# Three sines for four, a filter evacuated in 384 and 256 columns, an early table load, and a new time estimate and order for accumulating transfers in a gated long-convolution and token-mixer kernel

## The chip, the cores and the metric

The kernel runs on one core of one Trainium2 chip. The metric is the device time of one execution in microseconds (us). Before the change it took 180.29 us (median of 3 runs, 179.93 to 180.88). A profiled execution has a span some 2 us shorter than its time (177.7 and 179.50 us in the one profiled here). Each run also lists the mean clock granted to TensorE, as a share of full speed. Unless said, all runs told here are of the undisturbed (fast) state.

## The reference, cut to what matters

```python
x = A_q                                            # [1, 2048, 640], bf16
g = sigmoid((x * gate_w).sum(-1, keepdims=True))
# a: long convolution
kv = shift(k, shift_k) * v                         # 4-tap causal filter, then a product
y  = irfft(rfft(pad(kv)) * rfft(pad(ssm_k)))       # length 4096 per channel, first 2048 kept
a  = x * (y + kv * ssm_D)
# b: token mixer
b  = w2.T @ gelu(w1.T @ layernorm(x) + b1) + b2    # 2048 -> 1536 -> 2048 over the sequence
out = g * a + (1 - g) * b
```

## The kernel before

The Fourier transforms are matmuls against a basis of sines that the kernel computes itself (`FTB`), in four phases p, followed by additions on VectorE that combine the phases ("mixing"). A spectrum lies in four slots of 2560 columns of a tile `C[i]` or `SS`. The filter's spectrum (`W` evacuations) is made in two halves, then those of the two halves of kv. Products and cross sums of the spectra follow, then an inverse mixing and 64 + 64 inverse matmuls. TensorE fills all gaps with the mixer's two large matmuls: 384 of the first (`X,ring`), 384 of the second (`GT,W`).

All instructions are put down as operations in a list, with estimated durations. At build time a list scheduler simulates the engines, lets each take the ready operation of the lowest priority number, and so fixes the order in each engine's stream. On the chip each engine works through its stream in order, and stands at the first instruction whose operand isn't there. The scheduler's estimate for a transfer (those issued by GpSimd (POOL) accumulate: they add one tile to another while moving it):

```python
if e in ("SP", "QA") or op.lat < 0:                 # a transfer
    issue = 1.2 if e == "POOL" else 0.1
    s = max(t + issue, dma_free)
    dma_free = s + op.dur                           # one shared channel for all transfers
    op.end = dma_free + 2.0 + (6.0 if e == "POOL" else 0.0)   # accumulating ones land 6 us later
    free[e] = t + issue
```

The start of the kernel: four sines, five transposes of filter half one with spins (matmuls on a zero tile) ahead of them, and filter matmuls evacuated in 640 columns (2 x 320):

```python
for p in PORD:                                       # 0, 2, 1, 3
    t_ = tt("DVE", pv, V(tb, ...), V(jrow, 512 * p, ...), ALU.add)
    pprev = ts("DVE", pa, pa, 4095, None, ALU.bitwise_and, mode=4)
    sins[p] = act(FTB[:, p, ...], pa, ACT.Sin, bias=cst[:, 0:1], scale=..., name="sin")
...
def k_turn(hk):       # VectorE permutes a loaded block of k, a transfer then transposes it
    SC.add("DVE", 0.75, ... e.tensor_copy(ov, iv) ..., prio=0, name="kperm")
    dma(KT[hk // 2][...], o, 128 * 5120, rate=200.0, transpose=True, chain=True)
...
# the end: cross sums of the second half (A1), then the product of the first (A0)
acc_dma(A1[1], V1[1])                                # 2 accumulating transfers each
acc_dma(A1[0], V1[0])
chained(product, A0[1], A0[1], V0[1], H(V0[1], 0))   # ends with one more
lastacc = SC.ops[-1]
```

## Time and profile before

| | before |
|---|---|
| time, median of 3 (us) | 180.29 |
| span profiled (us), clock | 177.7, 1.000 |
| TensorE busy (us, share) | 172.6, 97% |
| VectorE busy | 169.7, 96% |
| ScalarE busy | 117.0, 66% |
| second mixer matmul starts (us) | 105.27 |
| VectorE's last mixing ends | 166.59 |

"Busy" is an engine's time in instructions. In the timelines below a row is: start, length, engine, line of the source, operation, output<-input with shapes, number of like instructions joined, and in brackets the idle time ahead of it and what ended it. In the lists of waits a row ends with the total, the number and the longest wait in us.

### The profile page before, as it was taken

Reading aid. Unit: us, or ns where it says so; the run is one execution under the profiler, and the core shown is the slowest. Engines: PE = TensorE matmul, PEld = TensorE weight load, DVE = VectorE, ACT = ScalarE, POOL = GpSimd, SP = SyncE. Lnnn points to the kernel's source line nnn. Section 1 sums busy time; section 2 is a strip of 40 time slices with the busy share of each in tenths; the row PEclk is TensorE's granted clock in tenths of the full one; section 3 lists DMA queues with packets and bytes.
Section 4 is the critical chain, followed back from the end, with each engine's and each line's share of the span. In section 5 each row is a group of like instructions: output and inputs, shape, how many; then the busy total and the mean of one; then the engine's idle time right before and its main releaser. Section 6 shows DMA issues by size and latency. Waiting matters only on the chain.

```text
span 177.7 us, 3342 instructions
## 1 busy us (share of the span) xinstructions
PE 172.6 (97%) x1380; PEld 129.4 (73%) x1381; DVE 169.7 (96%) x203; ACT 117.0 (66%) x176; POOL 43.6 (25%) x52
## 2 busy tenths in 40 slices
PE   7999999799999999999999999999999999999993
PEld 2666787487788776777777778888888887777772
DVE  7899789989999999999999999999999999999974
ACT  4999997998999999529999911231321323754760
POOL 8089803300000065000241101204343000252000
PEclk9999999999999999999999999999999999999999
DMA  4999999999999999999999998898999999499363
GB/s 136 394 411 374 391 312 156 248 414 374 191 240 315 109 216 226 231 228 278 230 227 271 205 248 299 144 225 230 188 193 217 207 218 408 167 197 212 93 241 131
DMA packets 38542, 43.51 MB, mean 245 GB/s; under 512 B 15867, under 2 KB 31360, under 8 KB 38528
## 3 DMA queue, kind: packets, MB, share of 16 engines
q1 hardware_dynamic: 33296, 32.16, 61.2%
q0 software_dynamic: 5200, 11.14, 36.5%
q8 instruction: 11, 0.18, 0.5%
q14 instruction: 3, 0.02, 0.0%
q10 hardware_dynamic: 32, 0.01, 0.0%
HBM read 25.87 MB, written 2.62 MB: 160 GB/s over the span
## 4 chain that ended last, share of the span: by engine, by line
PE 88%; DMA 5%; ACT 3%; SPq 2%; issue 0%; DVE 0%
PE pp L298 88%; DMA rows<-in_B_b_dram 5%; SPq L272 2%; ACT C L676 1%; ACT L676 1%; ACT GT L676 0%; DVE O L688 0%
## 5 line engine op out<-in xcount | busy, mean ns | idle before, releaser
L298 PE MATMUL pp<-X,ring 128*128 128x320 bf16 x384 | 55.3, 299 | 0.0
L632 DVE TENSOR_TENSOR C<-C 128x2560 bf16<-128x2560 bf16 (+2 forms) x37 | 54.5, 1523 | 0.8 <-ACT C L676 0.6
L298 PE MATMUL pp<-GT,W 128*128 128x320 bf16 x384 | 52.6, 299 | 0.0
L298 PEld LDWEIGHTS pp<-GT,W 128*128 128x128 bf16 x384 | 43.5, 113 | 8.7
L298 PEld LDWEIGHTS pp<-X,ring 128*128 128x128 bf16 x384 | 37.3, 98 | 14.3
L676 ACT ACTIVATE C<-pp 128x640 bf16<-128x640 f32 x64 | 40.7, 731 | 2.8 <-PE pp L298 2.7
L676 ACT ACTIVATE O<-pp,c,omg 128x640 bf16<-128x640 f32 x15 | 13.3, 885 | 34.7 <-PE pp L298 34.7
L267 POOL DMA_DIRECT2D C<-C x8 | 11.0, 1616 | 43.9 <-DVE C L632 43.9
L298 PE MATMUL pp<-wT,FTB 128*128 128x320 bf16 x112 | 17.1, 299 | 0.7 <-ACT GT L676 0.5
L676 ACT ACTIVATE cgb<-pp,gg 128x640 bf16<-128x640 f32 x16 | 12.7, 795 | 5.6 <-PE pp L298 5.2
L676 ACT ACTIVATE GT<-pp,cc 128x640 bf16<-128x640 f32 x12 | 9.6, 803 | 9.3 <-PE pp L298 9.2
L298 PEld LDWEIGHTS pp<-wT,FTB 128*128 128x128 bf16 x112 | 10.5, 98 | 5.6 <-ACT GT L676 0.8
L632 DVE TENSOR_TENSOR tm<-C,C 128x2560 bf16<-128x2560 bf16 (+1 forms) x7 | 14.3, 2059 | 0.0
L954 DVE BATCH_NORM_STATS2 stats<-X 128x6 f32<-128x320 bf16 x32 | 13.6, 464 | 0.5 <-DMA X<-in_A_q_dram 0.5
L298 PE MATMUL pp<-C,FTB 128*128 128x320 bf16 x96 | 13.4, 299 | 0.0
L267 POOL DMA_DIRECT2D C<-q_hi x6 | 5.9, 977 | 27.6 <-DVE C L632 12.9
L298 PEld LDWEIGHTS pp<-C,FTB 128*128 128x128 bf16 x96 | 9.4, 98 | 3.6
L676 ACT ACTIVATE gq<-gq 128x640 bf16<-128x640 bf16 x16 | 11.8, 745 | 0.2 <-DVE gq L632 0.2
L632 DVE TENSOR_TENSOR SS<-C 128x2560 bf16<-128x2560 bf16 x8 | 11.7, 1488 | 0.1
L632 DVE TENSOR_TENSOR C<-tm 128x2560 bf16<-128x2560 bf16 (+1 forms) x9 | 10.7, 1194 | 0.1
L676 ACT ACTIVATE ksh<-pp 128x1024 bf16<-128x1024 f32 (+1 forms) x12 | 9.9, 903 | 0.2 <-PE pp L298 0.2
L267 POOL DMA_DIRECT2D O<-q_hi x4 | 4.8, 1200 | 21.3 <-DVE q_hi L632 21.3
(77 smaller groups left out, 197.0 us busy)
## 6 DMA issues: line engine op xcount, KB each, us to landing
ring<-in_B_w_dram SPq DMA_DIRECT2D x12, 512.0 KB, 12.2
W<-in_B_w_dram SPq DMA_DIRECT2D x12, 512.0 KB, 5.5
C<-C POOLq DMA_DIRECT2D x8, 640.0 KB, 11.5
X<-in_A_q_dram SPq DMA_DIRECT2D x4, 640.0 KB, 8.4
kn<-in_A_k_dram SPq DMA_DIRECT2D x4, 640.0 KB, 9.4
out_dram<-O SPq DMA_DIRECT2D x7, 320.0 KB, 3.4
C<-SS POOLq DMA_DIRECT2D x3, 640.0 KB, 11.9
ssm<-in_A_ssm_k_dram SPq DMA_DIRECT2D x3, 512.0 KB, 6.8
```

What stands on the lines that cost most here:

```text
L267: ins = engobj.dma_start(out_ap, in_ap, accum_op=ALU.add, max_dma_last_dim=2560)
L272: ins = engobj.dma_start(out_ap, in_ap)
L298: ins = self.nc.tensor.matmul(ps_ap, lhsT=lhsT, rhs=rhs, start=start, stop=stop, skip_group_check=True)
L632: o_ = SC.add(eng, d, lambda s: T.op(eng, lambda e: e.tensor_tensor(o, a, b, op), rd, [o]), rd, [o], prio=prio, name="tt")
L676: return T.op("ACT", lambda e: e.activation(o, src, func, **kw), rr + [src], ww)
L954: ops.append(SC.add("DVE", 0.38, (lambda o, i: lambda s: T.op("DVE", lambda e: e.bn_stats(o, i), [i], [o]))(o, i), [i], [o]))
```

## The change

Its intent: shorten the start, which ScalarE bounds (one sine less, the basis of phases 0 and 2 from one sine by copies and negations; fewer evacuations), take the gelu table's load out of a queue where TensorE waits for it, place the first two turns of k where their loads have landed, and order the accumulating transfers of the end so that the first cross sum needed isn't queued behind others. Cut to its core:

```diff
-                    s = max(t + issue, dma_free)
-                    dma_free = s + op.dur
-                    op.end = dma_free + 2.0 + (6.0 if e == "POOL" else 0.0)
+                    if e == "POOL":
+                        acc_free = max(t + issue + 0.6, acc_free) + 2.2 * op.dur
+                        op.end = acc_free
+                    else:
+                        s = max(t + issue, dma_free)
+                        dma_free = s + op.dur
+                        op.end = dma_free + 2.0
...
-        SPIN = (7, 3, 3, 2, 2)
+        SPIN = (7, 2, 1, 1, 1)
...
-            sins[p] = act(FTB[:, p, ...], pa, ACT.Sin, ...)            # x4
+            sins[(0, 1, 3)[n_]] = act(so, si, ACT.Sin, ...)            # x3
+        sins[2] = sins[0]
+        for o_, i_, sg in (...):                                       # 4 scalings by -1 or 1
+            h_ = ts("DVE", V(FTB, o_[0], ...), V(FTB, i_[0], ...), sg, None, ALU.mult, mode=4)
...
+            if ci == 1:          # one evacuation of 4 x 256 columns per phase
+                ... wT[:, kt, p, 384:640] ...
-                items.append((chk(c), ..., srcW(0)(kt, p, ci), ...))   # 320 columns
+                items.append((..., wT[:, kt, p, 0:384], ...))          # 384 columns
...
+                g_ = act(gws[:, :], cst[:, 1:2], ACT.Gelu_apprx_tanh, name="tab", prio=SC.ops[-1].idx)
+                g_.after.add(SC.ops[-2])
...
+                        if t in (13, 15):
+                            kpos.append(b1)
                     k_turn(hk)
+                    SC.ops[-2].after.add(kpos[hk])
...
+        n_acc = len(SC.ops)
         acc_dma(A1[1], V1[1])
         acc_dma(A1[0], V1[0])
         chained(product, A0[1], A0[1], V0[1], H(V0[1], 0))
         lastacc = SC.ops[-1]
+        for o_ in SC.ops[n_acc:]:
+            if o_.eng == "POOL" and o_ is not lastacc:
+                o_.after.add(lastacc)
```

Below, "the new model" is the first hunk and "the reorder" the last; the rest are "the early parts".

More of the change, by code (lines that the diff above doesn't have):

```diff
@@ L405, in run @@
         dma_free = 0.3
+        acc_free = 0.0
         avail = {}
@@ L809, in _build @@
         iota(acol[:, :], [[0, 1]], 0, 8)
-        jr = lambda p, kt: iota(jrow[:, 2 * p + kt, :], [[-512 * (4 * kt + p), 2], [4 * (4 * kt + p), 128]], 4096 + 4 * kt + p, 0)
-        for p in PORD:
-            for kt in range(2):
-                jr(p, kt).dur = 0.34
-            if p == PORD[0]:
-                iota(dif[:, :], [[1, 128]], 0, -1)
+        for k_, j in enumerate((0, 4, 2, 6)):
+            iota(jrow[:, k_, 0:128], [[4 * j, 128]], 4096 + j, 0).dur = 0.23
+        iota(dif[:, :], [[1, 128]], 0, -1)
+        for k_, j in enumerate((1, 5, 3, 7)):
+            iota(jrow[:, 4 + k_, :], [[-512 * j, 2], [4 * j, 128]], 4096 + j, 0).dur = 0.34
         iota(dif2[:, :], [[1, 32]], 128, -1)
@@ L823, in _build @@
         sins = {}
-        for p in PORD:
-            pv = V(pint, 1024 * p, [[512, 2], [256, 2], [1, 256]])
-            t_ = tt("DVE", pv, V(tb, 0, [[0, 2], [256, 2], [1, 256]]), V(jrow, 512 * p, [[256, 2], [0, 2], [1, 256]]), ALU.add)
-            if p != 0:
+        pprev = None
+        for n_ in range(3):
+            pa = V(pint, 1024 * n_, [[1, 1024]])
+            if n_ == 0:
+                t_ = tt("DVE", V(pint, 0, [[256, 4], [128, 2], [1, 128]]), V(tb, 0, [[0, 4], [256, 2], [1, 128]]), V(jrow, 0, [[256, 4], [0, 2], [1, 128]]), ALU.add)
+            else:
+                t_ = tt("DVE", V(pint, 1024 * n_, [[512, 2], [256, 2], [1, 256]]), V(tb, 0, [[0, 2], [256, 2], [1, 256]]), V(jrow, 1024 + 512 * (n_ - 1), [[256, 2], [0, 2], [1, 256]]), ALU.add)
                 t_.after.add(pprev)
-            pa = pint[:, p, :, :, :].rearrange("q a b c -> q (a b c)")
             pprev = ts("DVE", pa, pa, 4095, None, ALU.bitwise_and, mode=4)
-            if p == 0:
+            if n_ == 0:
                 ts("DVE", ident[:, :], dif[:, :], 0.0, None, ALU.is_equal)
-            sins[p] = act(FTB[:, p, :, :, :, :].rearrange("q a b c d -> q (a b c d)"), pa, ACT.Sin, bias=cst[:, 0:1],
-                scale=-(2.0 * math.pi / 4096.0) * (1.0 - 1e-6), name="sin")
+            so = V(FTB, 0, [[2048, 2], [256, 4], [1, 128]]) if n_ == 0 else V(FTB, 1024 * (1, 3)[n_ - 1], [[1, 1024]])
+            si = V(pint, 0, [[512, 2], [128, 4], [1, 128]]) if n_ == 0 else pa
+            sins[(0, 1, 3)[n_]] = act(so, si, ACT.Sin, bias=cst[:, 0:1], scale=-(2.0 * math.pi / 4096.0) * (1.0 - 1e-6), name="sin")
+        sins[2] = sins[0]
+        half_rows = []
+        for o_, i_, sg in (((640, 256), (512, 256), -1.0), ((128, 256), (0, 256), 1.0), ((2432, 256), (2048, 768), -1.0), ((2176, 768), (2304, 256), 1.0)):
+            h_ = ts("DVE", V(FTB, o_[0], [[o_[1], 2], [1, 128]]), V(FTB, i_[0], [[i_[1], 2], [1, 128]]), sg, None, ALU.mult, mode=4)
+            h_.after.add(pprev)
+            half_rows.append(h_)
         SC.add("DVE", 0.6, lambda s: T.op("DVE", lambda e: e.tensor_copy(ro, ri), [ri], [ro]), [ri], [ro], prio=0, name="taps")
@@ L872, in transp @@
             m_ = mms(vt, (spin(SPIN[db]) if h == 0 else []) + items, name="wtr")
-            m_.dur = (0.65 + 0.31 * SPIN[db] if h == 0 else 0.55)
+            m_.dur = (1.9 if db == 0 else 0.65 + 0.31 * SPIN[db]) if h == 0 else 0.55
             o_ = act(V(wT, 2 * h * SL + 128 * db, [[SL, 2], [D, 4], [1, 128]]), (lambda s: s[:, :].rearrange("q (a b c) -> q a b c", a=2, b=4)), ACT.Copy, vt=vt, name="wT")
             if h == 0:
-                o_.after.add(sins[0 if db == 0 else 2])
+                o_.after.add(sins[1 if db < 3 else 3])
+                if db == 2:
+                    sins[3].after.add(o_)
         def fwd_c(p, ci, dst, scale):
+            if ci == 1:
+                vt = _VT("cv")
+                items = []
+                for k2 in range(2):
+                    for c in range(2):
+                        for kt in range(2):
+                            items.append(((lambda s, j=2 * c + k2: s[:, 256 * j:256 * j + 256]), FTB[:, p, kt, c, k2, :], wT[:, kt, p, 384:640], kt == 0, kt == 1))
+                m_ = mms(vt, items, name="W")
+                m_.dur = 0.88
+                act(V(dst, p * SL + 384, [[D, 4], [1, 256]]), lambda s: s[:, :].rearrange("p (a f) -> p a f", a=4), ACT.Copy, vt=vt, name="We", scale=scale)
+                return
             for k2 in range(2):
@@ L883, in fwd_c @@
                     for c in range(2):
-                        items.append((chk(c), FTB[:, p, kt, c, k2, :], srcW(0)(kt, p, ci), kt == 0, kt == 1))
+                        items.append(((lambda s, c=c: s[:, 512 * c:512 * c + 384]), FTB[:, p, kt, c, k2, :], wT[:, kt, p, 0:384], kt == 0, kt == 1))
                 m_ = mms(vt, (spin(WSPIN) if (p, ci, k2) == (PORD[0], 0, 0) else []) + items, name="W")
-                m_.dur = 0.54
-                act(V(dst, p * SL + k2 * D + 320 * ci, [[2 * D, 2], [1, 320]]), two, ACT.Copy, vt=vt, name="We", scale=scale)
+                m_.dur = 0.66
+                act(V(dst, p * SL + k2 * D, [[2 * D, 2], [1, 384]]), lambda s: s[:, :].rearrange("p (c f) -> p c f", c=2)[:, :, 0:384], ACT.Copy, vt=vt, name="We", scale=scale)
         def fwd(src, h, p, dst, slot, scale, name, neg=lambda c, k2: False):
@@ L956, in ln_tile @@
                 ops[0].after.add(pprev)
+                ops[0].after.update(half_rows)
             o, i = mv[:, t, :], stats[:, t, :]
@@ L979, in _build @@
         KFP = (0, 5, 10, 15)
-        WSPIN = 3
+        WSPIN = 1
         srcW = lambda h: (lambda kt, p, ci: wT[:, 2 * h + kt, p, 320 * ci:320 * ci + 320])
@@ L986, in _build @@
                 consts()
+            else:
+                g_ = act(gws[:, :], cst[:, 1:2], ACT.Gelu_apprx_tanh, name="tab", prio=SC.ops[-1].idx)
+                g_.dur = 1.5
+                g_.after.add(SC.ops[-2])
             if h in (1,):
@@ L1008, in _build @@
                 pag = []
+                kpos = []
                 def flush():
```

## The prediction

> **What bounds the kernel now.** I read the page first. On the page of the kernel before, the shares of each engine and the chain that ended last say this (busy microseconds, share, instructions; then the chain's shares by engine):
>
> ```profile
> PE 172.6 (97%) x1380; PEld 129.4 (73%) x1381; DVE 169.7 (96%) x203; ACT 117.0 (66%) x176; POOL 43.6 (25%) x52
> ...
> PE 88%; DMA 5%; ACT 3%; SPq 2%; issue 0%; DVE 0%
> ```
>
> TensorE is the end's engine for 88% of the span, but VectorE is as full. So a gain must come from both, and the question is where either loses time. The table of stages (busy time of each engine in a stretch) tells where TensorE isn't full after its start:
>
> ```profile
> 20.50:33.20 12.70, 12.70 (x115) 9.67 (x112) 11.61 (x27) 11.15 (x15) 2.65 (x5) 1.00 1.23 256
> 33.20:35.10 1.90, 1.00 (x7) 0.33 (x7) 1.90 (x3) 1.90 (x4) 1.19 (x1) 1.00 1.06 238
> 35.10:147.80 112.70, 112.70 (x930) 87.51 (x930) 111.25 (x89) 70.71 (x116) 19.99 (x18) 1.00 1.04 239
> ```
>
> Only 33.2 to 35.1 us has a hole (1.00 of 1.90 busy, so 0.9 us lost); afterwards TensorE never stops. The timeline of ScalarE (start, length, operation) shows what is behind that hole and behind the start:
>
> ```profile
> 3.76 3.36 ACT L676 ACTIVATE FTB<-pint,cst 128x1024 bf16<-128x1024 int16 x3 [0.86 <-DVE pint L646]
> 7.03 1.00 ACT L676 ACTIVATE wT<-pp 128x1024 bf16<-128x1024 f32 x1
> 7.93 1.14 ACT L676 ACTIVATE FTB<-pint,cst 128x1024 bf16<-128x1024 int16 x1
> ...
> 9.14 3.76 ACT L676 ACTIVATE wT<-pp 128x1024 bf16<-128x1024 f32 x4
> ...
> 14.33 7.86 ACT L676 ACTIVATE C<-pp 128x640 bf16<-128x640 f32 x13
> 22.49 0.70 ACT L676 ACTIVATE C<-pp 128x640 bf16<-128x640 f32 x1 [0.31 <-PE pp L298]
> ...
> 28.66 1.30 ACT L676 ACTIVATE C<-pp 128x640 bf16<-128x640 f32 x2 [0.88 <-PE pp L298]
> ...
> 31.60 1.28 ACT L676 ACT_TABLE_LOAD   x1
> 32.90 0.79 ACT L676 ACTIVATE GT<-pp,cc 128x640 bf16<-128x640 f32 x1
> ```
>
> From 3.76 to 23.19 us ScalarE has no gap but 0.31 us: the start is ScalarE's. TensorE looks busy in it, but 12 of its matmuls between 4.3 and 12 us are spins on a zero tile, which only keep it running. The gelu's table is loaded at 31.60 with evacuations queued behind it. The waits of TensorE and VectorE are the other half:
>
> ```profile
> DVE kp L764 <- DMA kn<-in_A_k_dram: 1.3, 2, 1.1
> ...
> PE pp L298 <- ACT GT L676: 0.5, 1, 0.5
> PE pp L298 <- ACT C L676: 0.4, 2, 0.2
> DVE C L632 <- ACT C L676: 0.6, 1, 0.6
> DVE stats L954 <- DMA X<-in_A_q_dram: 0.5, 1, 0.5
> ```
>
> The two PE lines are the hole of 0.9 us. The 0.6 us of VectorE (at 36.1) comes from the same queue of ScalarE. The 1.1 us is VectorE standing at 21.6 us in front of the first turn of k, which was put in its stream before the load of k had landed.
>
> **What the skill says.** The Trainium skill, "ScalarE: Activation LUTs", section "What ACT_TABLE_LOAD costs", gives about 1283 ns for a load, and some 1.4 us of drain on top. The trace agrees with the first (1.28) and shows no second: gelu starts at 32.90, 1.30 after the load began. The section "Table sets" says that copy is in every set, so copies after the tiny gelu need no table; the trace agrees, with two loads only and copies after each. "VectorE: DVE Perf Modes", section "The perf-mode tier table", lets a 16-bit tensor-scalar run at up to 4x and a tensor-tensor at 2x: the trace has 0.43 us for the 1024-element AND and 0.69 for the 1024-element add. "TensorE: Matmul & The Clock Gate", section "What's actually happening", has the array start at half rate until about 3.4 us of work: the first 7 spins took 3.17 us (0.43 each at the pace of the stream) and the next 3 took 0.81, so the trace agrees. That bears on the spins that go.
>
> **The change part by part.**
>
> *Sines.* The basis of phases 0 and 2 is half redundant: its other half is the computed half copied or negated. One sine of 1024 covers the distinct halves of both; four sines become three. Three in 3.36 us is 1.12 each, so ScalarE saves **1.12 us**. VectorE loses one add and one AND (0.68 and 0.43, some 1.05 at the stream's pace: the next add starts at 3.65, its successor at 4.79) and gets four scalings of 256 elements; I estimate 0.16 each from the 0.43 of 1024, so 0.64. Net 0.4 us, but VectorE then stands before the load of X (0.5 us of wait at 7.70 already), so this is worth nothing to it.
>
> *Filter half one.* Before, 16 evacuations of 640 columns; 13 in 7.86 is 0.605 each, 9.68 in all. After, 8 of 768 and 4 of 1024. From 0.605 at 640 and 0.94 at 1024 (4 in 3.76), a line gives 0.717 at 768: 8 x 0.717 + 4 x 0.94 = 9.50. So **0.2 us**. Matmul columns are the same: 64 x 320 = 32 x 384 + 32 x 256 = 20480. The 384 columns need just the first three transposed blocks, and the fourth sine goes behind their evacuation, so the filter's matmuls can start some 2 us before today's 11.77. ScalarE is full from 3.76 in any case, so its end of this stage moves by 1.12 + 0.2 = **1.3 us**. Until layer-normed X is there (first X matmuls at 20.66; its chain on VectorE begins with the load at 7.70, which doesn't move), TensorE has nothing else to fill with. ScalarE's 1.3 us is two evacuations' worth, 8 matmuls of 0.137 (48 of them took 6.69): 1.1 to **1.2 us** of TensorE work brought forward.
>
> *Spins.* 7 fewer, each 0.216 at full rate (1.5 us), all in stretches where TensorE waits for ScalarE: nothing by itself.
>
> *Gelu table.* The load goes ahead, near the last transposes of half two (ScalarE at about 27), where ScalarE has 0.88 us idle at 27.8. The load leaves the queue at 31.6. I count the whole **0.9 us** hole of TensorE and up to 0.65 of VectorE's wait.
>
> *k turn.* The first turn now comes after the statistics of tile 13, so VectorE does normalisation instead of standing: **1.05 us** of VectorE. The transposes of k on the queue start perhaps 0.2 us later than today's 23.53; they landed at 33.9 before their matmuls at 35.02, so there is 1 us of room.
>
> *Cross sums.* The four accumulating transfers of A1 now follow the one of A0, which today is issued here:
>
> ```profile
> 122.98 2.93 POOL L267 DMA_DIRECT2D C<-C  x2
> 131.21 1.20 POOL L267 DMA_DIRECT2D C<-SS  x1 [5.30 <-DVE C L632]
> 131.94 2.94 POOL L267 DMA_DIRECT2D C<-C  x2
> ```
>
> Two move from 122.98 to behind 131.21. The one of A0 (9.9 us to landing) meets less traffic; the others had 8.5 to 14.3. With all four after 132 the last lands, by an estimate of 4 x 4 to 5 us after 133, at 149 to 153. Their readers, the second inverse mixing, start at 152.95. No gain, a little risk. The change in the scheduler's model of these transfers only changes orders.
>
> *Sum.* TensorE 1.2 + 0.9 = 2.1 us. VectorE 1.05 + 0.65 + 0.27 (its wait for rstd, if it goes) = 2.0 at most. At the end both count: the second inverse's last inputs come from VectorE at 166.6, and behind them lie 4.5 us of inverse matmuls and 3.4 us of last mixer matmuls. If TensorE gains but VectorE doesn't, TensorE burns its reserve (40 mixer matmuls at 157.4) and the end moves by perhaps 0.5 us. So the gain is near VectorE's. I take two thirds of 2.0 to 2.1 as surviving the reshuffled order: **1.4 us, 180.3 - 1.4 = 178.9 us**.
>
> **Rivals.** (1) VectorE gives the gain back: the second load of k at 39.94 landed just when VectorE came (0.2 us of wait). If VectorE comes 1.5 us earlier and the order puts the turn there, it stands, since that load is bound by the queue behind the transposes. Against it: other mixing is there to be ordered ahead. Then 179.8. (2) The clock: fewer spins leave TensorE idler from 5 to 12 us; if the array falls back to half rate, filter matmuls of 384 take over twice ScalarE's time and 1 to 2 us are lost: 180 to 180.5. Against it: the filter's matmuls start earlier and replace spins. (3) The constants' transposes stand in TensorE's stream before a load that landed at 13.98 (0.6 us of wait); with everything else earlier, that fixed landing may cost more. 0.3 us. (4) Late accumulations hold VectorE near 153; the reserve hides up to 2 us: 0 to 1 us. (5) All parts pay, with earlier LN besides: 177.5.
>
> **Range and chances.** The spread from 177.5 (rival 5) to 180.3 (rivals 1 or 2 eating all) is what the parts allow; 8 in 10 for **177.6 to 180.3**. Faster by 2% needs under 176.7, 3.6 us, more than every hole I can name: 0.04. Slower by 2% needs a new stall of over 5 us: 0.02. Within 2%: 0.94.
>
> **What would show it.** In the changed profile: three sines; the last filter evacuation of half one ending near 21.9 instead of 23.2; filter matmuls from about 9.5; the second table load before 29 and no TensorE hole at 33 to 35; no VectorE wait of 1 us for k at 22; VectorE's long mixing stream starting 1 to 2 us earlier, and its last mixing ending near 165 instead of 166.6. I'd be wrong if VectorE's waits for k, for accumulated tiles, or for evacuations grow by over 1 us, if matmuls of 384 columns run at half rate after 9 us, or if the end no longer follows VectorE's last mixing.

## More of the kernel before

Transfers issued by GpSimd (POOL) accumulate: they add one tile to another while moving it, which takes additions off VectorE. The mixing of the last spectrum uses two of them.

```python
def mixing_acc(R, Th, Ts):                          # R = C[3]
    for i in range(2):
        tt("DVE", sl(Th, Ts + i), sl(R, i), sl(R, 2 + i), ALU.subtract)
        dma(pr(R, i), pr(R, 2 + i), 128 * 5120, stream="POOL", prio=0, accum=True)
    tt("DVE", sl(R, 2), sl(R, 0), sl(R, 1), ALU.add)          # reads both landings
    tt("DVE", sl(R, 3), sl(R, 0), sl(R, 1), ALU.subtract)
    ...
for g in range(2):
    cross(g)      # products of the halves' spectra: VectorE work that doesn't need C[3]
```

## The result

The changed kernel took **183.16 us** (median of 4, 182.98 to 183.92), the kernel before in the same rounds 180.45 (median of 4). The ratio is 1.0159, with a 95% interval of 1.0119 to 1.0200: slower by 1.6%, inside the 2% class but outside the predicted range of 177.6 to 180.3. A ratio here is the mean time of one kernel's fast runs over that of the other's of the same rounds, so it isn't quite the ratio of the medians quoted.

The page of the changed kernel: busy time, TensorE's slices (tenths busy, then its granted clock), and the chain that ended last.

```profile
PE 172.5 (95%) x1373; PEld 129.3 (71%) x1374; DVE 169.2 (93%) x205; ACT 116.1 (64%) x172; POOL 42.3 (23%) x52
...
PE   7899999999899999999999999999999957999994
...
PEclk9999999999999999999999999999999996999999
...
DVE 51%; PE 21%; DMA 15%; ACT 5%; issue 4%; SPq 2%; POOL 1%; DVEq 0%
```

TensorE and VectorE are busy for as long as before, to 0.5 us, in a span 3.7 us longer. So most of the loss is waiting. (For TensorE the equality is partly chance: seven spins less, and later a stretch at half clock.) The slices show where: TensorE has a dip (5, 7) at the 33rd and 34th of 40, about 145 to 154 us, and its clock falls there. And the chain is no longer TensorE's (it had 88% of it) but VectorE's, with a transfer in it. VectorE's waits in the changed kernel:

```profile
DVE C L637 <- DMA C<-C: 2.9, 1, 2.9
DVE kp L769 <- DMA kn<-in_A_k_dram: 2.0, 2, 1.6
```

The first is new. VectorE's timeline around it:

```profile
92.89 1.49 DVE L637 TENSOR_TENSOR tm<-C,C 128x2560 bf16<-128x2560 bf16 x1
94.95 0.17 DVE L637 TENSOR_TENSOR gth<-sd,gacc 128x16 f32<-128x16 f32 x1 [0.57 <-ACT gq L681]
97.98 1.49 DVE L637 TENSOR_TENSOR C<-C 128x2560 bf16<-128x2560 bf16 x1 [2.86 <-DMA C<-C]
```

The addition at 97.98 is the one of `mixing_acc` that reads both landings. It stands in the stream right behind the small gate product at 94.95, so VectorE does nothing for 2.86 us. In the kernel before, the same addition in VectorE's timeline:

```profile
100.45 0.82 DVE L632 TENSOR_TENSOR C<-tm 128x1280 bf16<-128x1280 bf16 x1
101.19 1.49 DVE L632 TENSOR_TENSOR C<-C 128x2560 bf16<-128x2560 bf16 x1
```

There three cross products of four operations each stand ahead of it, and it waits for nothing; in the changed kernel only one and the first operation of the second do. The chain of the changed kernel, in order of time, leads the wait back to the second accumulating transfer:

```profile
84.36 1.15 POOL C L267
...
86.02 11.88 DMA C<-C
...
97.98 1.49 DVE C L637
```

GpSimd's timeline of the kernel before has the same two issues:

```profile
84.90 1.20 POOL L267 DMA_DIRECT2D C<-C  x1 [14.39 <-DVE C L632]
88.83 1.20 POOL L267 DMA_DIRECT2D C<-C  x1 [2.73 <-DVE C L632]
```

From issue to landing the four took, by the lists of transfers, 8.1 us (84.36) and 11.9 us (86.02) after the change, and 7.2 us (84.90) and 10.7 us (88.83) before it. The second transfer is issued 2.8 us earlier than before and lands at 97.9 instead of 99.5. The scheduler's own plan (what it believes, no time of the chip; printed when the kernel is built, and in no trace) says why the addition moved. With the old model it plans landings at 95.64 and 100.31 and puts three cross products ahead of the addition. With the new one 640 KB have op.dur = 655360 B / 365 B per ns = 1.795 us, so the first transfer takes 1.2 + 0.6 + 2.2 x 1.795 = 5.75 us and a queued one 3.95 us more: landings at 89.90 and 93.85, the addition at 94.41. The chip's second landing came 4.0 us later than that plan.

What follows from 2.86 us on VectorE is seen 50 us later. TensorE's timeline of the end, before and then after:

```profile
148.73 8.86 PE L298 MATMUL pp<-C,FTB 128*128 128x320 bf16 x64
157.43 5.60 PE L298 MATMUL pp<-GT,W 128*128 128x320 bf16 x40
...
171.55 3.42 PE L298 MATMUL pp<-GT,W 128*128 128x320 bf16 x24
```

```profile
150.82 10.53 PE L298 MATMUL pp<-C,FTB 128*128 128x320 bf16 x64 [2.98 <-DVE C L637]
161.18 5.60 PE L298 MATMUL pp<-GT,W 128*128 128x320 bf16 x40
...
175.31 3.42 PE L298 MATMUL pp<-GT,W 128*128 128x320 bf16 x24
```

TensorE waits 2.98 us for the first inverse mixing, and then runs the 64 inverse matmuls in 10.53 us instead of 8.86. The table of stages shows the clock (after the stage: PE, PEld, DVE, ACT, POOL busy; then the granted clock, the DMA share, GB/s):

```profile
147.80:150.80 3.00, 0.04 (x1) 0.01 (x1) 3.00 (x3) 0.00 (x0) 0.00 (x0) 1.00 1.06 306
150.80:152.20 1.40, 1.38 (x8) 0.82 (x9) 1.36 (x2) 0.00 (x0) 0.00 (x0) 0.72 1.06 293
152.20:154.50 2.30, 2.30 (x11) 1.31 (x10) 2.30 (x2) 0.80 (x1) 0.00 (x0) 0.50 1.11 212
```

After the hole the clock fell to 0.50 at about 151.4 us (0.72 is the mean over that stretch) and came back at about 154.8. VectorE's own last mixing, before and after:

```profile
163.69 2.90 DVE L632 TENSOR_TENSOR SS<-C 128x2560 bf16<-128x2560 bf16 x2
```

```profile
167.28 2.89 DVE L637 TENSOR_TENSOR SS<-C 128x2560 bf16<-128x2560 bf16 x2
```

It is 3.6 us later, and so is the end (3.76 us between the last rows of TensorE). Two paths are late by the same amount here, so the trace alone doesn't tell whether VectorE's lateness or TensorE's hole with its half clock sets the end.

The start, on the other hand, went as intended. ScalarE's timeline of the changed kernel:

```profile
3.68 2.21 ACT L681 ACTIVATE FTB<-pint,cst 128x1024 bf16<-128x1024 int16 x2 [0.78 <-DVE pint L651]
...
14.24 7.29 ACT L681 ACTIVATE C<-pp 128x768 bf16<-128x768 f32 x9
21.36 4.76 ACT L681 ACTIVATE wT<-pp 128x1024 bf16<-128x1024 f32 x5
26.14 1.28 ACT L681 ACT_TABLE_LOAD   x1
27.43 0.20 ACT L681 ACTIVATE gws<-cst 128x1 f32<-128x1 f32 x1
```

The filter's half one is done at 21.36 instead of 23.09, the table is loaded at 26.14 instead of 31.60, and TensorE's hole at 33 to 35 us is gone; its second mixer matmul starts at 104.20 instead of 105.27. But VectorE lost most of its lead again at the third turn of k. Its timeline, before and after:

```profile
39.94 0.83 DVE L764 COPY kp<-kn 128x2560 bf16<-128x2560 bf16 x1 [0.21 <-DMA kn<-in_A_k_dram]
```

```profile
34.33 3.63 DVE L637 TENSOR_TENSOR C<-C 128x1280 bf16<-128x1280 bf16 x3
39.53 0.83 DVE L769 COPY kp<-kn 128x2560 bf16<-128x2560 bf16 x1 [1.56 <-DMA kn<-in_A_k_dram]
```

The mixing at 34.33 was at 36.10 before: 1.77 us ahead. At the turn of k only 0.41 us is left, since the load lands where it did.

### The profile page after: what moved, and what is told of

It reads as the page before. It is cut to its first block, busy times and chain, and to the rows that moved or that the text cites. A ratio compares the mean times of both kernels' runs of the same rounds, so it can differ in the third digit from the quotient of the medians.

```text
span 181.4 us, 3326 instructions
## 1 busy us (share of the span) xinstructions
PE 172.5 (95%) x1373; PEld 129.3 (71%) x1374; DVE 169.2 (93%) x205; ACT 116.1 (64%) x172; POOL 42.3 (23%) x52
## 4 chain that ended last, share of the span: by engine, by line
DVE 51%; PE 21%; DMA 15%; ACT 5%; issue 4%; SPq 2%; POOL 1%; DVEq 0%
DVE C L637 32%; PE pp L298 21%; DVE tm L637 9%; DMA C<-C 7%; DMA rows<-in_B_b_dram 5%; ACT C L681 4%; DMA kn<-in_A_k_dram 4%; DVE q_hi L637 3%; SPq L272 2%; DVE vkv L637 2%; DVE SS L637 2%; DVE kv L637 2%; DVE gq L637 1%; ACT wT L681 1%; POOL C L267 1%
## 5 line engine op out<-in xcount | busy, mean ns | idle before, releaser
L681 ACT ACTIVATE C<-pp 128x640 bf16<-128x640 f32 (+2 forms) x60 | 40.0, 757 | 3.9 <-PE pp L298 3.9
L267 POOL DMA_DIRECT2D C<-C x8 | 10.5, 1866 | 43.0 <-DVE C L637 42.6
L298 PE MATMUL pp<-C,FTB 128*128 128x320 bf16 x96 | 15.0, 322 | 3.0 <-DVE C L637 3.0
L298 PE MATMUL pp<-wT,FTB 128*128 128x320 bf16 (+2 forms) x112 | 16.5, 299 | 0.0
L298 PEld LDWEIGHTS pp<-C,FTB 128*128 128x128 bf16 x96 | 10.0, 104 | 7.9 <-issue 3.5
L681 ACT ACTIVATE wT<-pp 128x1024 bf16<-128x1024 f32 x10 | 9.6, 1066 | 0.1
```

The costliest lines, as they stand in the source:

```text
L267: ins = engobj.dma_start(out_ap, in_ap, accum_op=ALU.add, max_dma_last_dim=2560)
L298: ins = self.nc.tensor.matmul(ps_ap, lhsT=lhsT, rhs=rhs, start=start, stop=stop, skip_group_check=True)
L681: return T.op("ACT", lambda e: e.activation(o, src, func, **kw), rr + [src], ww)
```

## The experiments

**The theory.** The new model is too optimistic for these transfers, the addition was therefore placed too early, and its 2.86 us wait on VectorE, which is in order, is the whole loss. Rivals: the hole and half clock of TensorE near 150 us are the loss; the reorder delays the cross sums; one of the early parts costs something. The runs were made in three batches of four; each batch has its own runs of the kernel before, with medians of 179.92, 180.11 and 180.39 us.

### First batch: which part loses the time

**The addition alone moved.** The changed kernel with both of VectorE's operations on the landed sum placed behind the second cross product. Read against the changed kernel, TensorE's stream is identical, VectorE's differs only between the gate product and the cross products behind it, and ScalarE's by one gate operation.

```diff
-            tt("DVE", sl(R, 2), sl(R, 0), sl(R, 1), ALU.add)
-            tt("DVE", sl(R, 3), sl(R, 0), sl(R, 1), ALU.subtract)
+            held.append(tt("DVE", sl(R, 2), sl(R, 0), sl(R, 1), ALU.add))
+            held.append(tt("DVE", sl(R, 3), sl(R, 0), sl(R, 1), ALU.subtract))
 ...
         for g in range(2):
             cross(g)
+            if g == 0:
+                for o_ in held:
+                    o_.after.add(SC.ops[-2])
```

> The changed kernel, with one edit: VectorE's two mixing operations that read the tiles of the two accumulating transfers issued at 84.4 and 86.0 us go behind the second cross sum, so that 3 to 4 us of other work stands ahead of them; TensorE's order is the same. Theory A (the wait of 2.9 us for the accumulating transfer at 95 us pushed VectorE's whole later stream back, and everything else of the loss follows from it): no VectorE wait for a transfer at 95 us, no TensorE hole of 3.0 us at 147.8, no half-rate stretch behind it, about 179 us (183.2 less 3.0 of hole less 1.3 of half rate). Rival B (the accumulations of A1, moved behind the one of A0, or the tighter early part are what costs): VectorE waits later instead, and the time stays above 181.5 us.

Measured: 179.32 us (179.17 to 181.15), ratio to before 0.9982 (0.9926 to 1.0038). VectorE's timeline of this run:

```profile
95.22 0.17 DVE L637 TENSOR_TENSOR gth<-sd,gacc 128x16 f32<-128x16 f32 x1 [0.56 <-ACT gq L681]
95.31 0.82 DVE L637 TENSOR_TENSOR q_hi<-C,C 128x1280 bf16<-128x1280 bf16 x1
...
97.88 1.49 DVE L637 TENSOR_TENSOR C<-C 128x2560 bf16<-128x2560 bf16 x1
```

The addition runs at 97.88, as late as in the changed kernel, but cross work stands ahead of it and nothing waits. The hole of TensorE and the low clock are gone too (span's clock 1.000). So the whole loss of 1.6% comes from where these VectorE instructions stand.

**The old transfer model put back, the rest kept.**

```diff
-                    if e == "POOL":
-                        acc_free = max(t + issue + 0.6, acc_free) + 2.2 * op.dur
-                        op.end = acc_free
-                    ...
+                    s = max(t + issue, dma_free)
+                    dma_free = s + op.dur
+                    op.end = dma_free + 2.0 + (6.0 if e == "POOL" else 0.0)
```

> The changed kernel with the scheduler's old estimate of accumulating transfers (about 11 us from issue to landing, instead of 5.75 for the first and 3.95 more behind another); all other parts of the change stay. Theory A: 178.5 to 179.5 us, VectorE's waits for transfers of C at most 0.3 us. Rival B: the estimate only shuffles; still over 181.5 us.

Measured: 181.05 us (180.74 to 181.22), ratio 1.0058 (1.0022 to 1.0094). Better than the changed kernel, but not the 178.5 to 179.5 expected. The wait for the first accumulation is gone and another has come, for the reordered cross sums of A1. VectorE's timeline:

```profile
154.94 1.49 DVE L633 TENSOR_TENSOR SS<-C 128x2560 bf16<-128x2560 bf16 x1 [1.75 <-DMA C<-C]
```

The four transfers of A1 were issued from 132.09 right behind that of A0, and took 16.3 us to land (median). This is the "late accumulations" rival of the prediction. The order of TensorE's tail had changed too: 52 mixer matmuls between the two inverses and 12 behind the last, instead of 40 and 24. What that costs is taken up below.

**The new model alone, on the kernel before.** The reverse edit, nothing else.

> The kernel before with only the new estimate of accumulating transfers. Theory A: the mixing add is put ahead of the landing (measured 7 to 12 us after issue), so VectorE waits some 4 us at 95 us, and, as the accumulation of A0 is now issued last, perhaps again before the first inverse mixing: 183.5 to 188 us. Rival B: within 0.7 us of the kernel before.

Measured: 188.97 us (188.86 to 190.13), ratio 1.0509 (1.0466 to 1.0552): slower by 5.1%, a little more than expected. Its VectorE waits:

```profile
DVE C L637 <- DMA C<-C: 5.0, 1, 5.0
DVE C L637 <- DMA C<-SS: 2.6, 1, 2.6
```

No instruction was added or removed; only the belief about landing times differs. The prediction had said of this edit that it "only changes orders". It does, and the orders cost 5%.

**The hole filled.** To test the rival of hole and half clock, the changed kernel was made to run 24 more mixer matmuls ahead of the first inverse, which fills the hole.

```diff
-                    mms(vt, items, prio=2 * 10 ** 6 + 4 * (4 * n_ + p) + a, name="m2")
+                    m2s.append(mms(vt, items, prio=2 * 10 ** 6 + 4 * (4 * n_ + p) + a, name="m2"))
 ...
-                    mms(vt, items, name="inv")
+                    i_ = mms(vt, items, name="inv")
+                    if h == 0:
+                        i_.after.add(m2s[42])
```

> The changed kernel with the inverse products of half one put three groups of eight mixer matmuls (3.3 us) later in TensorE's stream, so that the hole at 147.8 us is filled; VectorE's wait at 95 us stays. Theory A (VectorE's lateness is the cost; the hole and the half clock are only how it shows, and TensorE's reserve of mixer work would have covered a part): no half-rate stretch, 0.5 to 2 us better than the changed kernel, 181 to 182.5 us. Rival C (the order of TensorE's stream is the whole loss): about 179 us.

Measured: 183.96 us (183.12 to 184.80), ratio 1.0216 (1.0170 to 1.0262). No gain at all: neither the 181 to 182.5 expected if VectorE's lateness is the cost and TensorE's reserve covers a part, nor the 179 if TensorE's order is the whole loss. TensorE's timeline:

```profile
152.79 8.85 PE L298 MATMUL pp<-C,FTB 128*128 128x320 bf16 x64 [0.42 <-DVE C L637]
...
165.37 4.51 PE L298 MATMUL pp<-C,FTB 128*128 128x320 bf16 x32 [2.64 <-DVE C L637]
```

The 64 inverse matmuls run at full speed (8.85 us), the hole has moved to the second inverse, and the time is no better: VectorE is late, and filling one of TensorE's holes only opens the next. This run doesn't price the half clock exactly, since its profile also had the first load of X 0.95 us later than that of the changed kernel and a new wait of 1.1 us for cross sums. But with no half clock left (1.00) the time is no better. In the changed kernel itself hole and half clock together could be worth some 1.4 us at most: TensorE reaches the last inverse block at 170.96, VectorE hasn't finished its input before 170.17, and of VectorE's lateness there 0.64 us are two waits for evacuations of the late inverse. That is less than half of the 3.7 us by which the span grew.

### Second batch: what the early parts are worth, and why the second run missed

**The third turn of k behind a mixing operation**, on top of the moved addition, so that VectorE doesn't stand 1.6 us at 38 us.

```diff
+            mix0 = SC.ops[m0:]                    # the operations of the first mixing
 ...
         for hk in range(2, 4):
             k_turn(hk)
+            if hk == 2:
+                turn2 = SC.ops[-2]
+                turn2.after.add(mix0[4])
 ...
             tt("DVE", o, kb[:, :, :], vi, ALU.mult, prio=0)
+            if hk == 0:
+                SC.ops[-1].after.add(turn2)
```

> The first experiment (mixing add behind the second cross sum), and the turn of the third k tile put behind one mixing operation of 1.4 us on VectorE, with the product that followed kept behind the turn. Theory (VectorE's gain of the first 35 us is eaten by its wait of 1.6 us for the load of k at 38 us, so the wanted gain of 1.4 us isn't seen): that wait falls under 0.4 us, VectorE's later stream is 1.2 to 1.4 us earlier, and the time is 178.0 us (177.6 to 178.6), about 1.2 us under the first experiment. Rival (VectorE's position is not what sets the end once nothing stalls): the same as the first experiment within 0.4 us.

Measured: 179.33 us (178.89 to 179.94), ratio 0.9965 (0.9927 to 1.0002). The expected 178.0 didn't come. VectorE's timeline says why:

```profile
39.96 0.83 DVE L769 COPY kp<-kn 128x2560 bf16<-128x2560 bf16 x1 [0.18 <-DMA kn<-in_A_k_dram]
41.54 0.83 DVE L769 COPY kp<-kn 128x2560 bf16<-128x2560 bf16 x1 [0.75 <-DMA kn<-in_A_k_dram]
```

The third turn waits only 0.18 us now, but the scheduler put the fourth right behind it, and that one waits 0.75. Most of the gain was turned into a new wait. With the addition moved alone the median was 179.32, in another batch; a difference isn't resolved.

**Old model and old order of the cross sums, early parts kept.** The second run's edit, and the reorder's loop removed.

```diff
-        for o_ in SC.ops[n_acc:]:
-            if o_.eng == "POOL" and o_ is not lastacc:
-                o_.after.add(lastacc)
```

> The changed kernel without its two scheduling parts: old estimate of accumulating transfers and old order of the A1 accumulations; sines, filter, spins, tiny gelu and k turn stay. Theory (the 1.7 us wait that the second experiment showed at 153 us is due to issuing the A1 accumulations behind the one of A0): that wait is gone, 179.0 to 179.8 us, like the first experiment. Rival (the early parts cost something late): stays at 180.5 to 181.

Measured: 180.95 us (180.02 to 181.20), ratio 1.0035 (0.9992 to 1.0079). No wait for an accumulation is left, and still it isn't the 179.0 to 179.8 expected. So the reorder wasn't the only reason for the miss of the second run. This profile has the same tail as there, in TensorE's timeline:

```profile
157.56 7.23 PE L298 MATMUL pp<-GT,W 128*128 128x320 bf16 x52
...
173.32 1.79 PE L298 MATMUL pp<-GT,W 128*128 128x320 bf16 x12
```

Twelve of the last mixer matmuls come ahead of the second inverse, where the kernel before has them behind it. Its start was also late in this profile; more on that at the end of the third batch.

**Only the early table load and the placed turns of k**, on the kernel before.

```diff
             if h == 0:
                 consts()
+            else:
+                g_ = act(gws[:, :], cst[:, 1:2], ACT.Gelu_apprx_tanh, name="tab", prio=SC.ops[-1].idx)
+                g_.dur = 1.5
+                g_.after.add(SC.ops[-2])
 ...
+                        if t in (13, 15):
+                            kpos.append(b1)
 ...
                     k_turn(hk)
+                    SC.ops[-2].after.add(kpos[hk])
```

> The kernel before with only the tiny gelu and the later first k turn. Theory: TensorE's hole of 0.9 us at 33 to 35 us is gone, VectorE's first k wait falls under 0.5, but the load of the third k tile is met earlier, wait over 1 us: 179.2 to 180.0 us, 0 to 0.6 us under the kernel before. If the sines and the filter are worth what I had put on them (1.2 us of TensorE work), this is 0.3 us or more slower than the kernel without model and reorder.

Measured: 179.79 us (179.31 to 180.25), ratio 0.9990 (0.9952 to 1.0027): inside the expected 179.2 to 180.0, and no gain beyond the noise. It is faster than the sixth run, not slower as the prediction's worth of the sines would have it, but the sixth has the other tail, so this doesn't price the sines. TensorE's hole at 33 us is gone, but VectorE waits 1.1 us for k and TensorE 1.1 us for the product `vkv` that follows from it.

**The tiny gelu left out**, on top of the moved addition.

```diff
-            else:
-                g_ = act(gws[:, :], cst[:, 1:2], ACT.Gelu_apprx_tanh, name="tab", prio=SC.ops[-1].idx)
-                g_.dur = 1.5
-                g_.after.add(SC.ops[-2])
```

> The first experiment without the tiny gelu; all orders but ScalarE's are the same. Theory: the table load stands in front of the first gelu again and TensorE has its hole of about 0.9 us near 33 us, but VectorE's 1.6 us wait for k hides its share, and TensorE has mixer work in reserve later: 0 to 0.5 us slower than the first experiment. Rival (the table load is the part that pays): 0.9 to 1.5 us slower.

Measured: 179.50 us (179.16 to 180.05), ratio 0.9978 (0.9941 to 1.0016), as with it. The hole is back in TensorE's waits and VectorE's wait for evacuations too:

```profile
PE pp L298 <- ACT GT L681: 0.8, 2, 0.6
```

```profile
DVE C L637 <- ACT C L681: 1.5, 2, 1.3
...
DVE kp L769 <- DMA kn<-in_A_k_dram: 0.6, 2, 0.4
```

VectorE's wait for k falls from 1.9 to 0.6 us in exchange for a longest wait of 1.3 us for evacuations. VectorE stands for about as long in both, once before the load of k and once before ScalarE.

### Third batch: the tail, the reorder, and a combination

**The tail kept as before**, on the kernel with old model and old order. Only TensorE's stream differs from that run: the last tile's 24 mixer matmuls are tied behind the last inverse, so that 40 and 24 come back for 52 and 12.

```diff
+                    i_ = mms(vt, items, name="inv")
+                    if h == 1 and p == 3 and kt == 1:
+                        m2s[-2].after.add(i_)
```

> The sixth experiment (no new estimate, no reorder) with one edit on TensorE alone: both parts of the mixer's last tile (24 matmuls) stay behind the last inverse product; there the scheduler had put 12 of them ahead of the second inverse. Theory (that placement is the loss of the sixth experiment: 12 matmuls of 0.137 us, 1.6 us, stand ahead of the inverse, and the tail of evacuation and VectorE work behind it has less to hide under): 1.2 to 1.7 us under the sixth experiment, 179.0 to 179.8 us. Rival (the sixth was slow because its loads landed late in the start): no difference over 0.5 us.

Measured: 179.38 us (179.00 to 179.86), ratio 0.9932 (0.9892 to 0.9972). The tail in TensorE's timeline:

```profile
156.77 5.60 PE L298 MATMUL pp<-GT,W 128*128 128x320 bf16 x40
...
170.94 3.42 PE L298 MATMUL pp<-GT,W 128*128 128x320 bf16 x24
```

The two runs are of different batches and differ in their ratios by 1.0%, in their medians by 1.57 us. The two profiles tell more: in the sixth run the first inverse starts 0.79 us later (148.87 and 148.08), since its start was late, but the second one 2.37 us later (164.62 and 162.25). So about 1.6 us, the time of twelve matmuls, arise at the tail: its order is the larger part of what kept the sixth run from its gain, and the late start another. And this run is the cleanest measure of the early parts: with the old model, the old order of the transfers and the old tail they are worth 0.7% (0.3 to 1.1).

**The reorder left out, the new model kept.**

```diff
-        for o_ in SC.ops[n_acc:]:
-            if o_.eng == "POOL" and o_ is not lastacc:
-                o_.after.add(lastacc)
```

> The changed kernel without the reorder of the cross sums only; the new estimate stays. Theory: the wait of 2.9 us at 95 us stays as it is, and the accumulation of A0, now issued behind the four of A1, lands too late for the first inverse mixing (as in the third experiment, wait 2.6 us), so 184.5 to 187 us; with the new estimate the reorder is a repair and no gain by itself. Rival (the reorder costs): 182 us or less.

Measured: 189.10 us (187.29 to 189.90), ratio 1.0454 (1.0387 to 1.0520); worse than expected, in the expected direction (its profile also has a late start, see below). VectorE's waits:

```profile
DVE C L637 <- DMA C<-SS: 4.1, 1, 4.1
DVE C L637 <- DMA C<-C: 2.2, 1, 2.2
```

The 4.1 us is for the transfer of A0. It was issued at 135.06 behind four others and landed 16.7 us later; in the changed kernel it goes first (134.03) and took 6.5. So under the new model the reorder is a repair: without it the same kernel is nearly 3% slower, and over 2% by its fastest run (187.29). Under the old model, where the scheduler put two of the four behind A0 anyway, it wasn't needed.

**Everything placed by hand**: the tail kept, and the third and fourth turns of k placed behind work that needs neither: the fifth run's lines for the third, and for the fourth

```diff
             if hk == 2:
                 turn2 = SC.ops[-2]
                 turn2.after.add(mix0[4])
+            else:
+                turn3 = SC.ops[-2]
 ...
             if hk == 0:
                 SC.ops[-1].after.add(turn2)
+                turn3.after.add(SC.ops[-1])
```

> The ninth experiment and the turns of the third and fourth k tile placed behind one mixing operation and behind the first product with v. Theory: VectorE's waits for k after 38 us sum to under 0.4 us, TensorE's stream isn't moved by it, so the end gains 0 to 0.8 us on the ninth: 178.4 to 179.4 us, and 0.5 to 1.0% under the kernel before. Rival (the later turn delays the transposes of k, and TensorE waits for them near 50 us by as much): no gain, TensorE wait for transposed k over 1 us.

Measured: 179.48 us over all six runs (178.39 to 181.27), ratio of the fast ones 0.9919 (0.9873 to 0.9966). The waits for k are gone from its profile. But the profiled execution was slow, with late loads (VectorE waits 2.6 us for X, and so comes late to every turn of k), so it doesn't show that the placement removed them, and its times are not used. It isn't distinguished from the run with the kept tail; both beat the kernel before by about 0.7 to 0.8%, and its best single run, 178.39 us, is the lowest.

**The rule for the first turns of k left out**, on top of the moved addition.

```diff
-                    SC.ops[-2].after.add(kpos[hk])
```

> The first experiment without the rule that puts the first k turns behind the statistics of tiles 13 and 15. Theory: VectorE waits about 1 us for the first k load at 22 us again, but arrives later at the third load and waits less there (0.5 us instead of 1.6), so the end doesn't move: within 0.5 us of the first experiment, 179.0 to 179.8 us. Rival (the turn is what pays): 0.8 us or more slower.

Measured: 180.70 us (179.31 to 181.47), ratio 0.9994 (0.9936 to 1.0052). Inconclusive: the interval reaches from 0.6% faster to 0.5% slower, and in its profile X landed at 8.69 us instead of 7.46, so that VectorE came to the turns of k too late to wait for any.

That landing is an open point for all small differences here. In the thirteen profiles of changed kernels the first statistics of X began between 7.44 and 9.31 us; the kernel before had 7.70. A single profile is thus good to about 1 us at the start, and the values of the early parts are taken from the timed rounds only.

The four latest of these (sixth, tenth, eleventh and twelfth run, 8.64 to 9.31 us) have something else in common: TensorE ran much of its start at half pace. A spin there took 0.61 to 0.63 us, in the changed kernel's profile 0.38. The pages of the tenth and eleventh run show it in the granted clock at their left end:

```profile
PEclk9759999999999999999999999999999995899999
```

```profile
PEclk9858999999999999999999999999999999999999
```

In the twelfth run the clock is listed as 1.00 and only the pace shows it. In these four the filter's half one ended at 23.04 to 24.68 us, instead of 21.36 in the changed kernel and 23.09 before, and VectorE waited 1.1 to 2.2 us for evacuations near 33 us: by that point such executions have lost the lead that the early parts gave. The other seven profiles with fewer spins kept the pace, and so did the three with the old number (the kernel before, the third and the seventh run), whose loads weren't as late. Whether late loads alone bring it about, or the missing spins with them, wasn't tested.

## Why the prediction was wrong, point by point

- **Three sines, and the filter in 384 and 256 columns.** Right in mechanism. ScalarE's half one ended 1.73 us earlier (1.3 predicted). The filter's matmuls started at 10.64 instead of 11.77, later than the 9.5 predicted: all five transposes still stand ahead of them in TensorE's stream, and one of these waits 0.55 us for the filter's load. TensorE had 1.07 us in hand at its second mixer matmul, where the prediction counted 2.1 with the gelu table.
- **Gelu table.** Right on the spot (load before 29 us, hole gone), wrong in worth. It counted 0.9 us for TensorE and 0.65 for VectorE; the run without the tiny gelu took the same time.
- **k turn.** Half right. The wait at 21.6 us of 1.05 us fell to 0.47. Rival 1, the third turn waiting at 40 us, came nearly in full: 0.21 became 1.56.
- **Spins and clock (rival 2).** In the changed kernel's profile the start kept its clock, so this isn't what made the result. But the rival isn't refuted: four of the eleven profiles with fewer spins ran much of the start at half pace (end of the third batch). In the changed kernel a half clock came at 151 us, behind the hole and not ahead of it.
- **The transfer model: the step that failed.** The prediction says that it "only changes orders" and gives the cross sums "no gain, a little risk". It looked at the reorder, whose landings it estimated at 149 to 153, and gave no number to the model's effect on the other transfers. It never asked which instruction waits for the two accumulations of the first mixing, and how much slack it had: in the trace of before the second landed at 88.83 + 10.7 = 99.5 and the addition came at 101.19, so 1.7 us of slack. The new model believes in 5.75 us for the first of the two, which took 7.2 in that very trace, and in 3.95 more for one queued behind it. Two others of 640 KB in that trace took 5.8 us (median), so the model fits some of these transfers, but not the pair that VectorE's next addition hangs on. That comparison could have been made blind. Rival 4 had a stall of this kind, "late accumulations", but at 153 us and hidden by the reserve; the list of signs had VectorE's waits for accumulated tiles growing by over 1 us, which is what came. Where the prediction has "only changes orders", the runs show 2.86 us of wait on VectorE; moving two instructions takes the whole 1.6% away, and the new model alone costs 5.1% on the kernel before.
- **The sum.** "1.4 us" of gain for the early parts wasn't far off: they are worth 0.7% (about 1.2 us) where the transfer model is left out and the tail's order kept. That nearness is partly luck: VectorE's 2.0 us were counted on the turn of k and the gelu table (and 0.27 for rstd), and these two alone gave 0.1% (0.9952 to 1.0027). Sines, filter and spins were never run alone, so which part pays is open. The term that was missing is about 4 us in the other direction.
- **The chance of a stall.** It held that slower by 2% "needs a new stall of over 5 us". VectorE and TensorE were both full, so each microsecond of a stall arrives at the end nearly whole: between 93 us, where VectorE was 0.65 us ahead of before, and its last mixing, 3.6 us behind, lie 4.25 us, of which 2.86 are this wait, 0.57 one for the gate's sum and 0.64 two for evacuations late in the tail.

Why the transfers are slower than the new model is argued and not shown. While the second one was under way, in the stretch from 85.6 to 87 us, the other queue's loads filled the transfer engines, by the changed kernel's table of queues (packets, MB, share of 16 engines):

```profile
q1 hardware_dynamic: 454, 0.45, 95.1%
```

The model's rate for an accumulating transfer has no term for loads beside it. Nor was the tail's order under the old model and the early parts (52 and 12) traced to one line of the change.

## What to carry to other kernels

In a kernel whose engine orders come from a simulated schedule, a change in an estimate is a change of the program: for each operation whose estimate moves, find its first reader in the trace and compare the measured landing with the new belief. An estimate that is too short can come back on an in-order engine as a wait (here 2.86 us for a landing 4.0 us later than planned); in the kernel before, the longer estimate left 1.7 us of slack and no wait. Where two engines are both nearly full, look first for new waits on the one that the chain that ended last runs through, and don't price a hole of the other engine until filling it has been tried.

## What the Trainium skill lacked or had wrong

- "DMA: Bandwidth & Descriptors", section "SWDGE vs HWDGE vs iDMA", says that an accumulating transfer must be issued from GpSimd, and gives no time for one. Here one of 640 KB inside the chip landed 5.8 to 8.8 us after its issue with none issued just ahead of it, 10.7 to 11.9 us as the second of two, and 14.0 to 16.7 us behind others in a row of five (medians where several are listed together).
- "TensorE: Matmul & The Clock Gate", section "What's actually happening", gives at least one idle window of about 3.4 us as what leads back to the half rate. Here a hole of 2.98 us was enough (clock 0.50 from about 151.4 to 154.8 us), and in the sixth run's profile one of 1.42 us, at 5.9 us, was followed by 0.50 from 8.2 to 11.6 us; one of 2.64 us in the fourth run was not (clock 1.00 throughout). The length of the hole alone doesn't decide here.
- "ScalarE: Activation LUTs", section "What ACT_TABLE_LOAD costs", adds some 1.38 us of drain to a load of 1.28 us. Here the next activation began 1.29 us after the load did (26.14 and 27.43), and the one ahead of the load had ended 0.02 us before it, so no drain was seen.
